# ScalarE's order in the first two groups of a retention and serf-MLP kernel, and the place of one chunk's masks

## The chip, the cores and the metric

The kernel runs on one core of one Trainium2 chip. The metric is the device time of one execution in microseconds (us); the kernel before has a median of 686.3 us over 9 runs (686.1 to 687.0). All times inside an execution are counted from the start of the profiled span.

## The reference

The inputs are q, k and v, each (4, 8, 768, 64): 4 sequences, 8 heads, 768 positions, 64 numbers per head, all float32. For each head with its own decay gamma, a state is updated position by position and read by the query:

```
state = gamma * state + k[t] v[t]^T
y[t]  = q[t] state / sqrt(64)
```

The heads' results side by side form x, with 3072 tokens and 512 columns. Then

```
h = x @ w_in                      # 512 -> 2048
g = h * erf(softplus(h))
out = g @ w_out                   # 2048 -> 512
```

The two weight matrices are float64 on the way in and are converted to float32 on the chip.

## The kernel before

**Chunks.** The retention is computed in 24 chunks of 128 positions (6 chunks in each of 4 sequences). For chunk j, `ret_scale` (K_, line 388) scales k and q with the decays on VectorE, `ret_transpose` (T, line 406) transposes both on TensorE and copies them to SBUF on ScalarE, `ret_scores` (S_, line 427) multiplies them into two PSUM banks, `ret_mask` (M, line 440) applies the causal mask on VectorE, `ret_out` (O_, line 450) multiplies with v and the state and copies the result into xT, and `ret_add` (A, line 606) adds the chunk's part to the state on VectorE. Outside the first stage all the banks called r come from a pool with two buffers: T, S_ and O_ each take both, and each waits until the readers of the one before are done. From chunk 6 on, k and q are loaded in another layout (kq and kb, `load`, line 100) by 32 small transfers and transposed on VectorE (line 413).

**The MLP.** The first 512 tokens (chunks 0 to 3) go through the MLP in groups g = 0 to 3 of four hidden tiles each (ft = 4g + u). `hidden` (line 669) computes one tile of 128 x 512 on TensorE into one of two banks called hp, and copies it to SBUF on ScalarE (line 682); a tile needs the bank of the tile two before it. `gate` (line 619) runs softplus over the group's four tiles, and for g > 0 erf right behind it; for g = 0 `gate_erf` (line 629) is called apart. Each of the two needs a table load on ScalarE. `gated` (line 650) multiplies with h on VectorE, and `project` (line 689) multiplies with w_out. Later tokens go in 256-token chunks through a scheme with seven products instead of eight (`hidden_part`, line 743; `project_part`, line 819); group 4 is the first of these. Its products use two hp banks: products 1, 6, 7 and 4 write the first, products 2, 5 and 3 the second. Product 2 is added to h on VectorE (line 770), and product 5 then overwrites its bank.

**The weights.** They arrive in 16 pieces, in the order in 0, in 1, in 2, in 3, out 0, out 1, in 4, in 5, out 2, out 3, in 6, in 7, out 4, out 5, out 6, out 7 (so piece 4 is out 0, and piece 10 is in 6). `conversion` (line 187) turns a piece into float32: exponent bits on VectorE (line 213), a Relu on ScalarE (line 214), mantissa (217), join with the low word (222), sign and exponent (225), final product (231). Once line 225 has read a piece, the transfer of the piece that takes its place is issued (`load_pieces_after`, line 181): piece 7 behind piece 3, piece 14 behind piece 10, piece 15 behind piece 12. Pieces 0 to 3 are converted in two parts, each of which serves one hidden tile; the others whole, in five steps (213 with 214; 217; 222; 225; 231), and the first step of the next piece goes between the third and the fourth from piece 5 on.

**What sets the order.** The program is written out in order by hand, and each engine and each issuing queue works in that order. Weight steps are put in between by a counter: `pace(n)` (line 277) adds n and issues as many steps as the counter then holds; operations that occupy VectorE subtract from it. `need(...)` (line 285) issues steps until a given weight block is done. The table `after` (line 913) says what follows each hidden tile at once (first list) and what waits until the middle of the next pacing (second list, run by `pace_around`, line 638). After (g, u) = (1, 0) the counter is set to 0. Nearly all transfers are issued from SyncE's queue, in program order: weight pieces, the chunks' loads (`load`), and `load_block_scales` (line 346), 17 small transfers that follow O_ of chunk 5.

Of the kernel before, what the change touches and what calls it, by code (L numbers as in the profile page):

```python
# [22 lines left out]
FG = 4  # L23
# [22 lines left out]
def kernel(  # L46
# [207 lines left out]
    def weights():  # L254


        pending = [conversion(n) for n in range(n_p)]
        begun = 0
        for n, steps in enumerate(pending):
            for k, _ in enumerate(steps, start=begun):  # L260
                yield
                if n > 4 and n + 1 < n_p and k == 2:
                    next(pending[n + 1])
                    yield
            begun = int(n > 4)
            if pieces[n] == ("out", 5):
                yield from sums("in", 0)
# [5 lines left out]
    weight_steps = weights()  # L273
# [11 lines left out]
    def need(*what):  # L285
        nonlocal room
        while what not in done:
            if next(weight_steps, done) is done:
                next(last_steps)
            room -= 1  # L290
# [315 lines left out]
    def ret_add(j):  # L606
        if j not in SU:
            return
        new = SU[j]
        if j % NC:  # L610
            nc.vector.tensor_tensor(state, state, new, op=ALU.add)
        else:
            nc.vector.tensor_copy(state, new)
        pace(-0.4)
# [23 lines left out]
    def pace_around(n):  # L638


        pace(n / 2)
        run(waiting)
        waiting.clear()
        pace(n / 2)
# [14 lines left out]
    def hidden_of(ft, t):  # L659

        if ft not in HP_:
            HP_[ft] = ps_h.tile([P, TCH], F32, name="hp")
        for kk in range(n_k):
            nc.tensor.matmul(  # L664
                HP_[ft][:, t], w_in_of(ft, kk), XC[0][:, kk, t],
                start=(kk == 0), stop=(kk == n_k - 1),
            )

    def hidden(g, u):
        ft = g * FG + u  # L670
        if u == 0:
            HS[g] = act.tile([P, N], F32, name="h")
        need("in", ft)
        if ft == 0:
            hidden_of(1, slice(TCH - C))
        hidden_of(ft, slice(TCH) if ft > 1 else slice(TCH - C, TCH))

        if ft < FG:
            need("in", ft + 2)
        if ft == 0:  # L680
            ret_add(JPC - 1)
        nc.scalar.copy(HS[g][:, u * TCH : (u + 1) * TCH], HP_.pop(ft))  # L682
        done.add(("hidden", ft))
        if ft == FG - 1:
            need("in", FG + 3)
        if g:
            pace_around(3.4 if ft > FG else 0)

# [155 lines left out]
    def put_part(m, step):  # L844
# [27 lines left out]
    K_, T, S_, M, O_, A = (  # L872
        ret_scale, ret_transpose, ret_scores, ret_mask, ret_out, ret_add
    )
# [6 lines left out]
    for j in range(JPC - 2):  # L881
# [3 lines left out]
        if j:  # L885
# [27 lines left out]
    after = [  # L913
        [([], [])] * FG,
        [
            ([(K_, 4), (next, weight_steps), (gate_erf, 0), (load, 5)], []),
            ([], []),
            ([(T, 4)], []),
            ([(S_, 4)], []),
        ],  # L920
        [
            ([(O_, 4)], [(A, 4)]),
            ([(T, 5)], []),
            ([(S_, 5)], [(M, 5)]),
            ([(O_, 5), (load_block_scales,)], [(A, 5)]),
        ],
        [
# [7 lines left out]
    for g in range(G0):  # L935
        for u in range(FG):

            if g and u == (2 if g == 1 else 0):
                waiting.append((gated, g - 1))
            hidden(g, u)  # L940
            run(after[g][u][0])
            if (g, u) == (1, 0):
                room = 0.0
            waiting.extend(after[g][u][1])
        gate(g)
        if g:
            for tt in range(TT):
                project(g - 1, tt)
                if g == 1 and tt < 2:
                    waiting.append((K_, 5) if tt else (M, 4))  # L950
                elif g == G0 - 1 and tt == 0:
                    waiting.extend([(K_, JPC + 2), (T, JPC + 2)])
                elif g == G0 - 1 and tt == 1:
                    load(JPC + 4)
                elif g == G0 - 1 and tt == 3:
                    K_(JPC + 3)
                    T(JPC + 3)
# [129 lines left out]
```

## Time and profile before

| what | value |
|---|---|
| median of 9 runs | 686.3 us (686.1 to 687.0) |
| profiled execution, its own time | 686.28 us |
| its span | 684.6 us |
| PE (TensorE matmul) busy | 677.0 us, 99% |
| PEld (TensorE weight load) busy | 578.3 us, 84% |
| DVE (VectorE) busy | 389.4 us, 57% |
| ACT (ScalarE) busy | 255.7 us, 37% |
| POOL (GpSimd) busy | 5.7 us, 1% |
| granted TensorE clock | 1.0 |
| chain that ended last | PE 90%, DVE 7%, issue 2%, ACT 1% |

A line of the timeline has the start in us, the time of the group, the engine, the source line, the operation, the tiles written and read with their shapes, and the number of instructions; in square brackets stands how long the engine stood idle before it, and what ended that. SPq is SyncE's issuing queue. Instructions on one engine overlap a little, so the distance from start to start is shorter than the sum of durations. Between 25 and 93 us VectorE is busy nearly without a break with the conversion of the weights; PE is busy except for a few holes.

### The profile page before, as it was taken

The page shows a single profiled execution, that of the slowest core. Times are in us where ns is not written, and L with a number is a line of the kernel's source. Part 1 is how long each engine was busy: PE and PEld are TensorE (multiplying, and loading weights), DVE is VectorE, ACT ScalarE, POOL GpSimd, SP SyncE. Part 2 cuts the span into 40 slices and gives each one's busy share as a digit, 9 for nine tenths or more (in the row PEclk, how much of TensorE's full clock was granted, in tenths as well). Part 3 has the DMA queues.
Part 4 walks back from the last instruction along what each step waited for, and adds up shares of the span by engine and source line. Part 5 has one row for each costly group of instructions (what it writes and reads, how often), then busy time and mean ns, then how long its engine had stood idle before and what let it go on. Part 6 is the DMA issues. An engine that isn't in the chain of part 4 may idle for free.

```text
span 684.6 us, 14442 instructions
## 1 busy us (share of the span) xinstructions
PE 677.0 (99%) x6214; PEld 578.3 (84%) x6214; DVE 389.4 (57%) x609; ACT 255.7 (37%) x291; POOL 5.7 (1%) x21
## 2 busy tenths in 40 slices
PE   9999999999999999999999999999999999999998
PEld 8744544586999999999999999999999999999996
DVE  4899999475945644543663564455544554343224
ACT  3368362415324234144143242341441432423431
POOL 2000000100000000000000000000000000000000
PEclk9999999999999999999999999999999999999999
DMA  9999743333412222221231222222312200000000
GB/s 193 214 237 256 181 139 90 63 60 61 108 35 43 75 41 39 74 44 33 66 56 33 65 44 45 70 41 44 72 35 47 51 27 1 2 32 1 1 32 32
DMA packets 156529, 47.65 MB, mean 70 GB/s; under 512 B 143025, under 2 KB 147377, under 8 KB 156465
## 3 DMA queue, kind: packets, MB, share of 16 engines
q1 hardware_dynamic: 153952, 46.19, 31.3%
q10 hardware_dynamic: 2512, 0.53, 0.5%
q8 instruction: 49, 0.80, 0.5%
q14 instruction: 16, 0.12, 0.1%
HBM read 40.39 MB, written 6.29 MB: 68 GB/s over the span
## 4 chain that ended last, share of the span: by engine, by line
PE 90%; DVE 7%; issue 2%; ACT 1%; POOL 0%; DVEq 0%; POOLq 0%
PE hp L757 37%; PE o L829 36%; PE o L700 6%; PE hp L664 3%; PE r L543 1%; PE hp L508 1%; PE o L579 1%; PE o L377 1%; DVE w_out_sb L217 1%; DVE w_out_sb L225 1%; DVE w_out_sb L222 1%; PE r L431 1%; DVE w_in_sb L225 1%; PE hp L558 1%; DVE w_in_sb L231 1%
## 5 line engine op out<-in xcount | busy, mean ns | idle before, releaser
L757 PE MATMUL hp<-xs,w_in_sb 128*128 128x128 f32 x1280 | 149.7, 275 | 0.0
L757 PEld LDWEIGHTS hp<-xs,w_in_sb 128*128 128x128 f32 x1280 | 147.8, 192 | 1.6 <-issue 0.5
L829 PE MATMUL o<-w_out_sb,h 128*128 128x256 f32 x640 | 141.7, 379 | 0.0
L829 PEld LDWEIGHTS o<-w_out_sb,h 128*128 128x128 f32 x640 | 121.6, 190 | 16.5
L757 PE MATMUL hp<-xT,w_in_sb 128*128 128x128 f32 x960 | 113.7, 275 | 0.0
L757 PEld LDWEIGHTS hp<-xT,w_in_sb 128*128 128x128 f32 x960 | 111.9, 192 | 1.9 <-issue 1.0
L829 PE MATMUL o<-w_out_sb,e 128*128 128x256 f32 x480 | 112.1, 383 | 0.0
L653 DVE TENSOR_TENSOR e<-h,e 128x1024 f32<-128x1024 f32 x42 | 49.6, 1221 | 101.7 <-ACT e L634 101.7
L829 PEld LDWEIGHTS o<-w_out_sb,e 128*128 128x128 f32 x480 | 88.2, 190 | 11.6
L664 PE MATMUL hp<-xT,w_in_sb 128*128 128x512 f32 (+2 forms) x144 | 57.2, 550 | 1.2 <-ACT h L682 1.2
L782 DVE TENSOR_TENSOR h<-h,hp 128x512 f32<-128x512 f32 x20 | 13.7, 687 | 75.1 <-PE hp L757 75.1
L624 ACT ACT_TABLE_LOAD x24 | 30.8, 1283 | 60.8 <-issue 45.4
L664 PEld LDWEIGHTS hp<-xT,w_in_sb 128*128 128x128 f32 x144 | 25.6, 190 | 28.5 <-issue 23.8
L634 ACT ACTIVATE e<-e 128x2048 f32<-128x2048 f32 (+1 forms) x23 | 42.1, 1836 | 0.2
L624 ACT ACTIVATE e<-h 128x2048 f32<-128x2048 f32 x22 | 42.0, 1910 | 0.2
L775 ACT COPY h<-hp 128x512 f32<-128x512 f32 x20 | 11.7, 585 | 61.1 <-PE hp L757 61.1
L780 ACT COPY h<-hp 128x512 f32<-128x512 f32 x20 | 11.7, 585 | 60.3 <-PE hp L757 60.3
L770 DVE TENSOR_TENSOR h<-h,hp 128x512 f32<-128x512 f32 x20 | 13.7, 685 | 35.7 <-PE hp L757 35.7
L773 ACT COPY h<-hp 128x512 f32<-128x512 f32 x20 | 11.7, 585 | 57.1 <-PE hp L757 57.1
L634 ACT ACT_TABLE_LOAD x24 | 30.8, 1283 | 0.4
L597 ACT COPY xT<-r 128x256 f32<-128x256 f32 x32 | 10.4, 375 | 54.8 <-PE r L543 54.8
L768 ACT COPY h<-hp 128x512 f32<-128x512 f32 x20 | 11.7, 587 | 48.6 <-PE hp L757 48.6
(136 smaller groups left out, 673.0 us busy)
## 6 DMA issues: line engine op xcount, KB each, us to landing
w_out_sb<-in_moe_w_out_dram SPq DMA_DIRECT2D x14, 512.0 KB, 5.1
kq<-in_k_dram SPq DMA_DIRECT2D x23, 256.0 KB, 3.8
v<-in_v_dram SPq DMA_DIRECT2D x23, 256.0 KB, 3.3
out_dram<-r SPq DMA_DIRECT2D x23, 256.0 KB, 2.9
kq<-in_q_dram SPq DMA_DIRECT2D x288, 16.0 KB, 1.8
kb<-in_k_dram SPq DMA_DIRECT2D x288, 16.0 KB, 1.7
w_in_sb<-in_moe_w_in_dram SPq DMA_DIRECT2D x8, 512.0 KB, 9.5
w_out_sb<-in_moe_w_in_dram SPq DMA_DIRECT2D x8, 256.0 KB, 8.9
```

Of the source, the lines that this page charges most:

```text
L225: nc.vector.scalar_tensor_tensor(power, hi, 1 << 31, power, op0=ALU.bitwise_and, op1=ALU.bitwise_or)
L624: nc.scalar.activation(E[g], HS[g], AF.Softplus)
L634: nc.scalar.activation(E[g][:, half], E[g][:, half], AF.Erf)
L653: nc.vector.tensor_tensor(E[g][:, half], HS[g][:, half], E[g][:, half], op=ALU.mult)
L664: nc.tensor.matmul(HP_[ft][:, t], w_in_of(ft, kk), XC[0][:, kk, t], start=(kk == 0), stop=(kk == n_k - 1),)
L700: nc.tensor.matmul(O[0][tt].rearrange("p (d c) -> p d c", d=2), E[g][:, u * TCH + tt * P : u * TCH + (tt + 1) * P], w_out_of(ft), start=(f ...
L757: nc.tensor.matmul(bank[:, u, :], w_in_sb[:, s, IN[a], kk, u * P : (u + 1) * P], XS[m][b][:, kk, :], start=(p in (1, 2, 5) and u == 0 and ...
L768: nc.scalar.copy(h["11"], flat)
L770: nc.vector.tensor_tensor(h["11"], h["11"], flat, op=ALU.add)
L773: nc.scalar.copy(h["12"], flat)
L782: nc.vector.tensor_tensor(h["12"], h["12"], flat, op=ALU.add)
L829: nc.tensor.matmul(O[m][i][:, half, :], G[g][a][:, u * P : (u + 1) * P], w_out_sb[:, s, OUT[b], u, :], start=i not in started, stop=(s == ...
```

## The change

Three edits of order; no instruction is added or taken out.

- After tile 3, `need` asks for the weights of tile 6 and not of tile 7. The second part of piece 3 (the weights of tile 7) is converted later: `need("in", 7)` stands behind the scaling of chunk 4, after tile 4. On ScalarE softplus of group 0 is now ahead of the Relu of that part.
- One weight step that stood behind the scaling of chunk 4 is dropped there (it comes with a later pacing), and erf of group 0 follows tile 5 instead of tile 4.
- The masks of chunk 5 follow its scores at once, and not in the middle of the pacing of tile 11.

```
         if ft == FG - 1:
-            need("in", FG + 3)
+            need("in", FG + 2)
...
         [
-            ([(K_, 4), (next, weight_steps), (gate_erf, 0), (load, 5)], []),
-            ([], []),
+            ([(K_, 4), (need, "in", FG + 3), (load, 5)], []),
+            ([(gate_erf, 0)], []),
             ([(T, 4)], []),
             ([(S_, 4)], []),
         ],
         [
             ([(O_, 4)], [(A, 4)]),
             ([(T, 5)], []),
-            ([(S_, 5)], [(M, 5)]),
+            ([(S_, 5), (M, 5)], []),
             ([(O_, 5), (load_block_scales,)], [(A, 5)]),
         ],
```

More of the change, by code (lines that the diff above doesn't have):

```diff
@@ L684, in hidden @@
         if ft == FG - 1:
-            need("in", FG + 3)
+            need("in", FG + 2)
         if g:
@@ L915 @@
         [
-            ([(K_, 4), (next, weight_steps), (gate_erf, 0), (load, 5)], []),
-            ([], []),
+            ([(K_, 4), (need, "in", FG + 3), (load, 5)], []),
+            ([(gate_erf, 0)], []),
             ([(T, 4)], []),
@@ L923 @@
             ([(T, 5)], []),
-            ([(S_, 5)], [(M, 5)]),
+            ([(S_, 5), (M, 5)], []),
             ([(O_, 5), (load_block_scales,)], [(A, 5)]),
```

## The prediction

> **What bounds the kernel now.** I read the page first: PE busy 99% of the span, and the chain that ended last is 90% PE, 7% DVE, 1% ACT. So time is lost only where PE stands still. The waits of PE from 22 us to 93 us have three entries: L664 on ACT's copies at L682 (1.2 us, twice), L431 on qT (0.8, before the change begins) and L471 on VectorE's masks at L443 (0.4, twice). After 93.19 us PE waits for nothing that the list shows, up to the end. Then I read the timeline, ScalarE first:
>
> ```profile
> 44.63 0.72 ACT L214 ACTIVATE w_in_sb<-w_in_sb,below 128x512 uint32<-128x512 uint32 x1 [2.01 <-DVE w_in_sb L213]
> 45.37 1.28 ACT L624 ACT_TABLE_LOAD   x1
> 46.66 1.91 ACT L624 ACTIVATE e<-h 128x2048 f32<-128x2048 f32 x1
> 48.48 0.57 ACT L682 COPY h<-hp 128x512 f32<-128x512 f32 x1
> 48.95 1.15 ACT L214 ACTIVATE w_out_sb<-w_out_sb,below 128x1024 uint32<-128x1024 uint32 x1
> 50.11 1.28 ACT L634 ACT_TABLE_LOAD   x1
> 51.41 1.92 ACT L634 ACTIVATE e<-e 128x2048 f32<-128x2048 f32 x1
> 53.23 1.05 ACT L682 COPY h<-hp 128x512 f32<-128x512 f32 x2
> ```
>
> The Relu of the last first-group weights (w_in piece 3, part 1) stands ahead of softplus; the copy of hidden tile 4 stands behind softplus, that of tile 5 behind erf. PE's side:
>
> ```profile
> 49.10 3.70 PE L664 MATMUL hp<-xT,w_in_sb 128*128 128x512 f32 x8 [1.06 <-ACT h L682]
> 52.64 1.04 PE L418 MATMUL r<-ident,kq 128*128 128x128 f32 x8
> 53.85 3.70 PE L664 MATMUL hp<-xT,w_in_sb 128*128 128x512 f32 x8 [0.17 <-ACT h L682]
> 57.48 1.16 PE L431 MATMUL r<-qT,kT 64*128 64x128 f32 x16
> ...
> 90.97 0.43 PE L471 MATMUL r<-qT,state 64*64 64x128 f32 x2 [0.23 <-DVE am L443]
> 91.57 0.66 PE L471 MATMUL r<-qT,state 64*64 64x128 f32 x14 [0.17 <-DVE am L443]
> ```
>
> Ends of matmuls are modelled and overlap, so I measure the loss from start to start. Tile 6 could start at 47.9 (tiles 1 to 5 run without a hole from 29.63 for 18.41 us, less the overlap of about 0.15 that later groups show): **1.2 lost**. T(4) to tile 7 takes 1.21 where T(5) to tile 10 takes 0.87: **0.34**. Tile 7 to S(4) takes 3.63 against 3.53: **0.1**. Tile 11 (87.05) to the end of L471 (92.16) takes 5.11, where 3.53 + 0.60 would do (75.93 to 76.53 in O(4)): **0.98**. In all 2.6 us.
>
> Last I read what PE's next partners do, since a PE that runs earlier meets them:
>
> ```profile
> 136.91 0.69 DVE L400 TENSOR_TENSOR kb<-kb,kq_b 128x512 f32<-128x512 f32 x1 [8.79 <-DMA kb<-in_k_dram]
> ...
> 139.34 0.65 DVE L770 TENSOR_TENSOR h<-h,hp 128x512 f32<-128x512 f32 x1
> 139.92 2.34 DVE L653 TENSOR_TENSOR r<-h,r 128x1024 f32<-128x1024 f32 x2
> ```
>
> VectorE waits 8.79 us for chunk 7's kb, then scales and transposes, then does L770, which reads the second hp bank of group 4. Product 5, whose matmuls overwrite that bank, starts on PE at 141.03. L770 ends at 139.99: **the slack is 1.0 us**, and it is the smallest I found behind 93 us. That kb comes off SyncE's queue, which issues without a pause:
>
> ```profile
> 89.09 0.88 SPq L174 DMA_DIRECT2D w_in_sb<-in_moe_w_out_dram  x2
> 90.01 8.87 SPq L350 DMA_DIRECT2D kq_b<-decay_k_dram  x16
> 98.92 0.43 SPq L354 DMA_DIRECT2D by_b<-decay_s_dram  x1
> 100.14 0.90 SPq L174 DMA_DIRECT2D w_out_sb<-in_moe_w_out_dram  x2
> 101.14 0.41 SPq L113 DMA_DIRECT2D kq<-in_k_dram  x1
> ```
>
> **Part 1: need 6 in place of 7, need 7 after K(4).** No instruction is added or removed; the five VectorE steps and one Relu of piece 3, part 1 move behind softplus and K(4), and the two loads of piece 7 that hang on them (46.28 on SP) move with them, with load(5) still behind. Softplus then follows the Relu of part 0 (41.89, 0.72): table 42.63, softplus 43.92, copy of tile 4 at 45.74 (1.82 after it, as at 48.48). PE needs that copy at 47.9, so the 1.2 goes. VectorE: K(4) at 44.17, piece 3's L213 at 45.30, its L222 at 46.08; its Relu waits for the copy and runs 46.21 to 46.93, so L225 starts at 46.97, not 46.69, and piece 4's L213 at 48.30 instead of 48.03: **+0.27 on VectorE**. Tile 7 needs these weights only at 52.3. Piece 7 is issued at 47.7, lands by 60.1 (12.4 as in this window), is read at 63: hidden, with 3 us left.
>
> **Part 2: the weight step dropped from (1,0), erf behind tile 5's copy.** The step is not lost: the pacing counter is set to 0 after (1,0), so each later place issues the same number of steps, and the whole sequence of weight steps runs one step late against everything else. Applied to the kernel before, this count gives VectorE's order in the trace exactly. ScalarE: copy of tile 5 at 48.06, Relu of piece 4 at 49.02 (behind L213), table 50.18, erf 51.48 to 53.40. gated(0) thus starts at 53.44 against 53.50, though one step less stands ahead of it: VectorE waits 0.29 there. Tile 5 is copied by 48.6, so the 0.34 goes; kT and qT are out by 54.9, as no Relu stands ahead of them. PE: tile 6 at 47.9, T(4) 51.44, tile 7 52.31, S(4) 55.84, project(0) at 56.93 instead of 58.57, and gated(0) (first half 54.7, second 55.8) is in time. Lead 1.64.
>
> A rule speaks against parts 1 and 2. The Trainium skill, "ScalarE: Activation LUTs", section "What ACT_TABLE_LOAD costs", adds about 1.38 us of drain to each switch of sets; here the load lasts 1.28 and softplus starts 1.29 after it, so the trace shows none. By the page tile 4's copy would come at 47.1, still before 47.9.
>
> **Part 3: M(5) right behind S(5).** The two masks pass three weight steps (piece 11's L213, piece 10's L225 and L231). VectorE, re-added with the start-to-start distances of the trace, is 0.32 late here (0.27 + 0.29, less 0.24 where M(4) and A(4) now fill gaps between dependent steps). So M(5) starts at 87.55 instead of 90.24 and ends at 88.83. But PE pays once before: T(5) takes the bank that A(4) (L611, 80.77 before) reads. A(4) now ends at 80.77 (80.36 + 0.41); PE would be there at 79.92 and starts T(5) at 80.81, a **new wait of 0.9**. S(5) at 85.2, tile 11 at 86.3, O(5) at 89.83 with the masks done, project(1) at 91.46 against 93.19. **Lead 1.7** (2.6 less 0.9).
>
> **What takes it back.** Piece 10's L225 releases piece 14's loads (89.09 on SP). It is now behind the masks: 1.20 + 0.32 = 1.5 later. The 18 issues behind it (kq_b, by_b) follow, so by_b ends at 100.86; 0.77 of slack ahead of piece 15's load (100.14) absorbs half, and load(6), load(7) and chunk 7's kb move by **0.75**. (Piece 15's own trigger is only 0.43 late.) L770 then ends at 140.74 and product 5 starts at 140.79 against 141.03. Behind it PE stays ahead of gated(3) (143.0 against 144.5) and of the rest. So of 1.7 us 0.24 remains: 686.28 - 0.24 = **686.0**, with 1.7 us between span and time as now (686.28 against 684.6). The profiled execution stands at the median of 686.3.
>
> The Trainium skill, "Perfetto Trace Analysis", section "Optimization Strategies", advises shortening what PE idles for. Taken alone that gives 684.6; the row at 136.91 with its slack of 1.0 gives 686.0.
>
> **Bounds of what no row shows.** The shift of SP's stream: at least about 0.2 (VectorE meets none of my waits and is 0.24 early: 1.20 - 0.24 - 0.77), so at most 0.8 gained; at most about 1.6 (VectorE 1.2 us late instead of 0.32, the length of two masks), so up to 0.6 lost. I take 0.75, which is re-added from rows. Loads of pieces 7 and 8 while the DMA engines are full (share over 1 until 72 us): nothing, to at most the 1.4 us by which the issue moves; I take nothing, since no VectorE row between 22 and 135 us waits for them.
>
> **Rivals.**
> - *The lead reaches the end.* It needs the kb chain to be no later than before and L770 not to hold product 5; PE's wait list, empty behind 93 us, speaks for it, the 8.79 us wait against. 686.28 - 1.7 = 684.6. Chance 0.08.
> - *Slower: SP's stream is later than PE's slack.* Place: piece 14's loads behind the masks of chunk 5. Each us that kb comes later than 1.0 is lost in full at product 5. With VectorE 1.2 late instead of 0.32 the stream is 1.6 late: 686.9; with VectorE 2.4 late, 2.8: 688.1. It decides from a piece-10 L225 ending 1.77 later than its 89.06; I have 1.5, so the margin is thin. Chance 0.14, half of it past 0.2%.
> - *It does not do what it says*: softplus stays late, or PE is held by the same copies: 686.3. Chance 0.06.
> - *Forecast*, product 5 held by L770 with a shift of 0.2 to 1.3: 685.5 to 686.6, likeliest 686.0. Chance 0.72.
>
> The range leaves out the full lead and the worst of the slower case: 685.1 to 687.0. 0.2% is 1.4 us, about what a measurement of this kernel can tell from no change: faster 0.08, same 0.85, slower 0.07.
>
> **What would show it.** Softplus near 43.9 and no wait at tiles 6 and 7; T(5) waiting for L611 near 80.8; masks near 87.6 and no wait at L471; project(1) near 91.5; piece 14's loads near 90.6, load(6) near 101.9, L400 near 137.7; product 5 waiting for L770. It is wrong if L400 starts no later than 137.0, or if PE runs through product 5 without a wait.

## The result, and the profile after

The changed kernel is **slower**: 689.49 us median of 9 runs (688.87 to 690.23) against 686.19 us for the kernel before (29 runs). The ratio is 1.0048, with a 95% interval of 1.0040 to 1.0057. The profiled execution took 689.08 us with a span of 687.4 us, 2.8 us more than the span before (684.6). Single runs of one kernel lie up to 4 us apart below, with a lower mean granted TensorE clock in the longer ones, and that is part of what is told.

The edits did what they were meant to do on PE. These are PE's lines from the timeline of the changed kernel (start, time, engine, line, what; in brackets PE's idle time and who ended it):

```profile
29.43 21.85 PE L664 MATMUL hp<-xT,w_in_sb 128*128 128x384 f32 x64
51.11 1.04 PE L418 MATMUL r<-ident,kq 128*128 128x128 f32 x8
51.99 3.60 PE L664 MATMUL hp<-xT,w_in_sb 128*128 128x512 f32 x8
...
80.66 0.66 PE L418 MATMUL r<-ident,kq 128*128 128x128 f32 x4 [0.47 <-DVE state L611]
...
89.41 0.67 PE L471 MATMUL r<-qT,state 64*64 64x128 f32 x16
...
91.03 14.00 PE L700 MATMUL o<-w_out_sb,r 128*128 128x512 f32 x32
...
137.78 1.16 PE L431 MATMUL r<-qT,kT 64*128 64x128 f32 x16
142.22 5.47 PE L757 MATMUL hp<-xs,w_in_sb 128*128 128x128 f32 x32 [3.27 <-DVE h L770]
147.52 3.60 PE L700 MATMUL o<-w_out_sb,r 128*128 128x512 f32 x8
```

The lines of the kernel before that these are compared with, PE's and one of SyncE's queue:

```profile
93.19 14.00 PE L700 MATMUL o<-w_out_sb,r 128*128 128x512 f32 x32
...
141.03 3.84 PE L757 MATMUL hp<-xs,w_in_sb 128*128 128x128 f32 x32
144.71 3.60 PE L700 MATMUL o<-w_out_sb,r 128*128 128x512 f32 x8
```

```profile
127.82 7.55 SPq L95 DMA_DIRECT2D kb<-in_k_dram  x16
```

Tiles 1 to 6 now run as one block of 64 matmuls, tile 7 follows T(4) without a hole, and L471 takes 0.67 us in one piece. project(1) starts at 91.03; before it was 93.19, so PE is 2.16 us ahead (0.2 of it from an earlier start of the block, 29.43 against 29.63). Then PE stands still for 3.27 us ahead of product 5, and the two products behind the stop take 5.30 us (142.22 to 147.52) where they took 3.68 (141.03 to 144.71). VectorE shows what it waited for:

```profile
139.08 0.69 DVE L400 TENSOR_TENSOR kb<-kb,kq_b 128x512 f32<-128x512 f32 x1 [10.75 <-DMA v<-in_v_dram]
...
141.51 0.65 DVE L770 TENSOR_TENSOR h<-h,hp 128x512 f32<-128x512 f32 x1
```

and SyncE's queue shows a part of why:

```profile
90.41 0.88 SPq L174 DMA_DIRECT2D w_in_sb<-in_moe_w_out_dram  x2
91.34 9.21 SPq L350 DMA_DIRECT2D kq_b<-decay_k_dram  x16
100.59 0.43 SPq L354 DMA_DIRECT2D by_b<-decay_s_dram  x1
101.12 0.90 SPq L174 DMA_DIRECT2D w_out_sb<-in_moe_w_out_dram  x2
102.12 0.41 SPq L113 DMA_DIRECT2D kq<-in_k_dram  x1
...
128.93 7.54 SPq L95 DMA_DIRECT2D kb<-in_k_dram  x16
136.52 0.43 SPq L122 DMA_DIRECT2D v<-in_v_dram  x1
137.05 1.27 SPq L113 DMA_DIRECT2D kq<-in_k_dram  x1
```

Piece 14's loads come 1.32 us later, load(6) 0.98 us, chunk 7's kb 1.11 us (127.82 before). L400 is later than that, by 2.17 us: the last kb transfers now took 3.0 us from issue to landing, against 1.9 before. (The bracket names v; the last kb transfer, issued at 136.04, landed 3.0 us later, at 139.04, so it is kb that ended the wait.)

The rest is the clock. In this table by stretches the columns are the stretch, its length, the busy time of PE, PEld, DVE, ACT and POOL with their counts, the clock granted to TensorE (1.00 is full speed), the DMA share and GB/s:

```profile
141.00:142.00 1.00, 0.00 (x0) 0.00 (x0) 1.00 (x2) 0.00 (x0) 0.00 (x0) 1.00 0.23 37
142.00:143.00 1.00, 0.78 (x7) 0.79 (x8) 1.00 (x2) 0.00 (x0) 0.00 (x0) 1.00 0.24 37
143.00:144.00 1.00, 1.00 (x8) 1.00 (x7) 1.00 (x2) 0.00 (x0) 0.00 (x0) 0.56 0.23 36
144.00:145.00 1.00, 1.00 (x7) 1.00 (x7) 1.00 (x3) 0.00 (x0) 0.00 (x0) 0.50 0.21 33
145.00:146.00 1.00, 1.00 (x6) 1.00 (x6) 1.00 (x3) 0.00 (x0) 0.00 (x0) 0.50 0.24 37
146.00:147.00 1.00, 1.00 (x9) 1.00 (x8) 0.97 (x2) 0.00 (x0) 0.00 (x0) 0.73 0.21 33
147.00:148.00 1.00, 1.00 (x9) 0.76 (x8) 1.00 (x1) 0.28 (x1) 0.00 (x0) 1.00 0.21 33
```

Nearly a microsecond after PE is back at work its clock is halved, for about 3.4 us. The sum closes on the profiled execution: product 5 starts 1.19 us later than before (142.22 against 141.03), the clock costs 1.62 (5.30 less 3.68), together 2.81, and the span grew by 2.8.

### The profile page after: what moved, and what is told of

Its sections match the earlier page's. It is cut to its first block, busy times and chain, and to the rows that moved or that the text cites. A ratio compares the mean times of both kernels' runs of the same rounds, so it can differ in the third digit from the quotient of the medians.

```text
span 687.4 us, 14444 instructions
## 1 busy us (share of the span) xinstructions
PE 677.6 (99%) x6214; PEld 579.6 (84%) x6214; DVE 389.5 (57%) x609; ACT 256.0 (37%) x291; POOL 5.7 (1%) x21
## 4 chain that ended last, share of the span: by engine, by line
PE 83%; DVE 6%; SPq 5%; issue 3%; DMA 2%; ACT 2%; POOL 0%; ACTq 0%; DVEq 0%; POOLq 0%
PE hp L757 36%; PE o L829 36%; SPq L95 4%; PE o L700 2%; PE r L543 1%; PE hp L508 1%; PE o L579 1%; PE hp L664 1%; PE o L377 1%; DMA kq<-in_k_dram 1%; DMA w_in_sb<-in_moe_w_out_dram 1%; DVE w_in_sb L225 1%; DVE w_out_sb L225 1%; PE r L431 1%; PE hp L558 1%
## 5 line engine op out<-in xcount | busy, mean ns | idle before, releaser
L757 PE MATMUL hp<-xs,w_in_sb 128*128 128x128 f32 x1280 | 151.3, 277 | 3.3 <-DVE h L770 3.3
L757 PEld LDWEIGHTS hp<-xs,w_in_sb 128*128 128x128 f32 x1280 | 149.4, 194 | 4.9 <-DVE h L770 3.5
L770 DVE TENSOR_TENSOR h<-h,hp 128x512 f32<-128x512 f32 x20 | 13.7, 685 | 35.7 <-PE hp L757 35.7
```

Of the source, the lines that this page charges most:

```text
L757: nc.tensor.matmul(bank[:, u, :], w_in_sb[:, s, IN[a], kk, u * P : (u + 1) * P], XS[m][b][:, kk, :], start=(p in (1, 2, 5) and u == 0 and ...
L770: nc.vector.tensor_tensor(h["11"], h["11"], flat, op=ALU.add)
```

## The experiments

**Theory.** PE's lead is real, but SyncE's stream and with it chunk 7's kb come later, so PE stops at product 5; the stop costs its length and then the clock. **Rival:** the changed order costs the time by itself, on ScalarE or through the weight steps that run one step late.

**1. ScalarE's order alone.** The changed kernel with the masks back in the pacing:

```
-            ([(S_, 5), (M, 5)], []),
+            ([(S_, 5)], [(M, 5)]),
```

> The two edits of ScalarE's order alone; the masks of chunk 5 stay in the pacing of tile 11. Theory (the loss comes from the masks ahead of piece 10's L225, which make SyncE's stream and chunk 7's kb late, while PE comes early to product 5): SyncE's stream moves by about 0.4 us at most, the masks stay near 90.5 so that PE's lead is given back at L471, product 5 waits at most a few tenths, no clock drop: 686.0 to 686.8. Rival (the order on ScalarE and the weights running one step late cost the time by themselves): 689, with the loss there although the masks are in their old place.

Measured: 689.34 us, ratio 1.0043 (1.0031 to 1.0055). The number is the rival's, and my expectation was wrong; the trace says why. Piece 14's loads are at 89.54, as good as in their old place, but piece 15's are at 101.71 (100.14 before), because of this VectorE line:

```profile
100.45 1.23 DVE L225 SCALAR_TENSOR_TENSOR w_out_sb<-w_out_sb 128x1024 uint32<-128x1024 uint32 x1 [0.99 <-ACT w_out_sb L214]
```

Piece 12's Relu stands on ScalarE behind softplus and erf of group 2. One step late is enough for that: its step now comes behind the gate of group 2 in the program, and before it came ahead of it. The Relu ran at 99.28, straight behind erf. In the changed kernel the same Relu also stands behind erf, but 1.24 us earlier (98.04), and no VectorE line waits for it. So the order on ScalarE alone makes SyncE's stream late by another way, load(6) at 102.70, and in the profiled run PE stops 1.75 us at product 5, with the clock halved behind it (one of the five runs, 688.16 us, has a mean clock of 1.0):

```profile
140.00:142.00 2.00, 0.30 (x6) 0.11 (x2) 2.00 (x5) 0.00 (x0) 0.00 (x0) 1.00 0.51 100
142.00:143.00 1.00, 0.95 (x5) 0.95 (x6) 1.00 (x1) 0.00 (x0) 0.00 (x0) 0.68 0.21 33
143.00:144.00 1.00, 1.00 (x7) 1.00 (x6) 1.00 (x2) 0.00 (x0) 0.00 (x0) 0.50 0.22 34
144.00:145.00 1.00, 1.00 (x7) 1.00 (x7) 1.00 (x3) 0.00 (x0) 0.00 (x0) 0.50 0.24 38
145.00:146.00 1.00, 1.00 (x7) 1.00 (x7) 1.00 (x2) 0.00 (x0) 0.00 (x0) 0.62 0.23 35
```

Whether the order does harm without the late stream is told by experiment 8.

**2. The masks alone.** The kernel before with `([(S_, 5), (M, 5)], [])`.

> The masks of chunk 5 at once, alone; ScalarE's order as in the kernel before. Theory: PE's lead at project(1) is 1.0 us (the hole ahead of L471 closes), piece 14's loads come 1.2 us later, SyncE's stream 0.45 us later; product 5 waits 0.4 us to 1.5 us (the more, the later the last kb transfer lands), and no clock drop since the stop is short: 685.6 to 686.8. Rival (ScalarE's order is the cause): also near 686, so it is told apart by the run with that order alone; if this run is near 689, the masks alone do it, without the lead of the first part.

Measured: 689.49 us median of 11 runs, ratio 1.0036 (1.0023 to 1.0049), in two bands: three runs of 686.12 to 687.10 with a mean granted clock of 1.0, and eight of 689.33 to 690.29 with 0.997 to 0.998. Two runs of the lower band lie in the expected range, the profiled one and the eight of the upper band above it: the expectation missed. The profiled run (687.10) is of the lower band, with piece 14's loads at 90.72, a stop of 1.21 us at product 5 and no clock drop. The mean clock of the upper band points to a drop, which was not expected; none of its runs has a profile, so how long PE stopped there is open.

**3. The changed kernel with SyncE's stream moved up.**

```
-            ([(O_, 4)], [(A, 4)]),
+            ([(O_, 4), (load_block_scales,)], [(A, 4)]),
...
-            ([(O_, 5), (load_block_scales,)], [(A, 5)]),
+            ([(O_, 5), (load, 6)], [(A, 5)]),
...
-            ([(load, 6)], []),
-            ([(load, 7)], []),
+            ([(load, 7)], []),
+            ([], []),
```

> The changed kernel with SyncE's stream moved up: the 17 block-scale transfers follow the output of chunk 4, and the loads of chunks 6 and 7 each stand one place earlier. Theory: chunk 7's kb lands some 8 us earlier, VectorE does not wait at L400 past 130 us, product 5 follows the scores of chunk 6 without a stop, the clock stays at 1.0, and PE's lead of 2.0 to 2.2 us reaches the end: 683.9 to 684.5. Rival (the loss is not SyncE's stream but the changed order itself, or another wait comes in its place): 686 or more.

Measured: **684.16 us**, ratio 0.9968 (0.9955 to 0.9981), five runs within 0.25 us. The kb of chunk 7 is there 7 us earlier than in the changed kernel, and product 5 follows the scores (PE first, then VectorE):

```profile
137.76 1.16 PE L431 MATMUL r<-qT,kT 64*128 64x128 f32 x16
138.85 3.84 PE L757 MATMUL hp<-xs,w_in_sb 128*128 128x128 f32 x32
142.53 3.60 PE L700 MATMUL o<-w_out_sb,r 128*128 128x512 f32 x8
```

```profile
131.83 0.69 DVE L400 TENSOR_TENSOR kb<-kb,kq_b 128x512 f32<-128x512 f32 x1 [1.68 <-DMA kb<-in_k_dram]
```

This is a kernel that beats both. It also gives the price list of the changed kernel: 684.09 (its profiled run) + 3.27 of stop + 1.62 of clock = 688.98, and 689.08 was measured.

**4. Products 5 and 7 of group 4 change places.** SyncE's stream is as late as in the changed kernel.

```
-        hidden_part(g, 5)
-        hidden_part(g, 7)
+        if first:
+            hidden_part(g, 7)
+            hidden_part(g, 5)
+            add_product_5(g)
+        else:
+            hidden_part(g, 5)
+            hidden_part(g, 7)
```

`add_product_5` is the addition on VectorE that stood behind product 7 and now follows product 5.

> The changed kernel, in which group 4 computes product 7 ahead of product 5 (its addition follows product 5); SyncE's stream is as late as in the changed kernel. Theory: PE has 1.8 us of work that needs no L770, so it stands still for 1.5 us and not 3.3, the granted clock stays at 1.0, and project(0) of group 3 starts near 144.5 instead of 147.5: 686.0 to 686.8, that is 3 us less than the changed kernel although only 1.8 us of work were moved. Rival (the clock drop has another cause than the length of the stop): the clock drops again and it is 687.5 or more.

Measured: 686.16 us (11 runs, 685.78 to 686.71), ratio 0.9997 (0.9988 to 1.0005): 3.3 us less than the changed kernel, from 2.0 us of work put into the stop. Between the two profiled runs it is 3.05 us: 1.45 of a shorter stop and 1.62 of clock. PE still waits 1.82 us for product 2's addition, but the clock stays up:

```profile
140.00:142.00 2.00, 0.74 (x7) 0.55 (x5) 2.00 (x5) 0.58 (x1) 0.00 (x0) 1.00 1.15 230
142.00:143.00 1.00, 0.43 (x3) 0.43 (x4) 1.00 (x2) 0.00 (x0) 0.00 (x0) 1.00 0.24 37
143.00:144.00 1.00, 1.00 (x11) 1.00 (x10) 1.00 (x2) 0.00 (x0) 0.00 (x0) 1.00 0.23 36
```

All 11 runs have a mean clock of 0.999 or 1.0. So the profiled run kept the clock behind a stop of 1.82 us, and that of experiment 1 lost it behind 1.75 us. What stands just ahead of the stop differs (2.0 us of product 7 here, 1.1 us of chunk 6's scores there); whether that decides was not tried.

**5. The kernel before with the stream moved up** as in experiment 3.

> The kernel before with SyncE's stream moved up in the same way (block scales behind the output of chunk 4, the loads of chunks 6 and 7 one place earlier). Theory: in the kernel before product 5 does not wait, so an earlier kb gives nothing: 686.0 to 686.4. Rival (the earlier loads themselves are the gain of the combined version): near 684.2, as much as with the changed order.

Measured: 686.35 us, ratio 1.0000 (0.9991 to 1.0009). The earlier loads alone give nothing.

**6 and 7. The kernel before with a late kb.** Five or nine small transfers ahead of chunk 7's loads, into a tile that nothing reads:

```
+        for i in range(5 if j == 7 else 0):
+            nc.sync.dma_start(
+                extra[:, i], decay_k[:, i % H : i % H + 1].rearrange("(a p) h -> p (a h)", p=32)
+            )
```

> The kernel before with 5 more transfers of 0.5 KB ahead of chunk 7's loads (decay numbers into a tile that nothing reads; about 0.55 us of SyncE's queue each, as the block scales take). Theory: kb comes 2.8 us later, 1.0 us of that is slack, so PE stands still for 1.8 us at product 5: 688.0 with the clock at 1.0 behind it, or 689.7 if a stop of that length already halves the clock for some 3.4 us. Rival (the late kb is harmless, the changed order costs the time): 686.3.

> The kernel before with 9 such transfers ahead of chunk 7's loads. Theory: kb comes 5.0 us later, PE stands still for 4.0 us at product 5, and the clock is halved behind it: 690.3 from the stop and 1.6 to 1.8 from the clock, 691.9 to 692.1. If the clock stays at 1.0, 690.3. Rival (the late kb is harmless): 686.3.

Measured with five: 687.55 us, ratio 1.0031 (1.0016 to 1.0046); eight runs at 687.24 to 687.57 with clock 1.0, four at 690.74 to 691.36 with 0.997 to 0.998. The transfers took 0.5 us each, and the kb stream starts 2.06 us later, not 2.8; the profiled run (687.49) stops 1.43 us, so about 0.6 to 1.0 us of the delay was slack (2.06 less 1.43, or by L400, which is 2.43 us later here, 2.43 less 1.43). Of the gap between the bands, 3.5 us, about half fits the clock: a mean of 0.9975 over 689 us is some 1.7 us lost, an estimate. What the other half is stays open, since no run of the upper band has a profile. Measured with nine: 692.93 us (four runs), ratio 1.0095 (1.0082 to 1.0108), above what I expected. PE stops 4.54 us, and the clock is at half for some 6.8 us, from about 144.8 to 151.6:

```profile
144.50:145.00 0.50, 0.00 (x0) 0.00 (x0) 0.50 (x2) 0.00 (x0) 0.00 (x0) 0.74 0.54 77
145.00:150.50 5.50, 5.08 (x24) 5.08 (x25) 5.47 (x7) 0.00 (x0) 0.00 (x0) 0.50 0.22 34
...
151.50:152.00 0.50, 0.50 (x6) 0.50 (x5) 0.00 (x0) 0.00 (x0) 0.00 (x0) 0.93 0.22 34
```

So a late kb alone, with the old order everywhere else, makes the same kind of loss, a stop at product 5 and the half clock behind it. The rival "the late kb is harmless" falls.

**8 and 9. Each part alone with the stream moved up.** Experiments 1 and 2 with the edit of experiment 3.

> ScalarE's order alone (masks of chunk 5 in their old place), with SyncE's stream moved up as in the combined version. Theory: with kb early nothing stops PE at product 5, and what this part is worth by itself shows: PE is 0.9 us ahead at project(1) in the run of this part with the late stream (92.38 with tiles 1 to 5 at the same start, against 93.19), so 685.3 to 685.6. Rival (this part is harmful in itself): 686.3 or more.

> The masks of chunk 5 at once alone, with SyncE's stream moved up. Theory: the hole of 1.0 us ahead of the output of chunk 5 is closed and reaches the end: 685.2 to 685.5; the clock stays at 1.0 in all runs, where the same kernel with the late stream fell into two bands of 686.1 to 687.1 and 689.3 to 690.3. Rival (the two bands come from the masks' place and not from the stop at product 5): two bands again.

Measured: ScalarE's order 685.26 us, ratio 0.9983 (0.9974 to 0.9992); the masks 685.30 us, ratio 0.9986 (0.9977 to 0.9995), in one band of 685.07 to 685.69. Each part is worth 1.0 to 1.1 us against the 686.33 of the same chip, together what experiment 3 gains. The rival falls: neither order does harm by itself. (The profiled run of the first, 686.38, is the longest of its 11; T(5) waits 1.47 us for L611 in it, and why longer than elsewhere is open.)

**10. The state's addition of chunk 4 at once**, on top of experiment 3: `([(O_, 4), (A, 4), (load_block_scales,)], [])`.

> The changed kernel with SyncE's stream moved up, and the state's addition of chunk 4 at once behind its output instead of in the pacing of tile 9. Theory (the transposes of chunk 5 wait for that addition, 0.5 us by the wait list and some 0.7 us from start to start): PE starts T(5) without a stop and project(1) comes up to 0.7 us earlier, which reaches the end: 683.3 to 683.8. Rival (the hole only moves, to the masks of chunk 5 or to the next addition): 684.1 or more.

Measured: **683.79 us**, ratio 0.9961 (0.9949 to 0.9973), the fastest of all. T(5) runs in one piece (tile 10 starts 0.87 us behind it, as in the kernel before) and PE's wait for L611 is gone. From the start of the block of tiles to project(1) PE takes 61.00 us, against 61.56 in experiment 3. The median is 0.37 us below that of experiment 3, but the two ran on different chips and the intervals of their ratios overlap, so the gain in time is not shown as firmly as the gain in the trace.

**11. The block scales alone moved up**, in the changed kernel.

```
-            ([(O_, 4)], [(A, 4)]),
+            ([(O_, 4), (load_block_scales,)], [(A, 4)]),
...
-            ([(O_, 5), (load_block_scales,)], [(A, 5)]),
+            ([(O_, 5)], [(A, 5)]),
```

> The changed kernel with the block scales alone moved up (behind the output of chunk 4); the loads of chunks 6 and 7 keep their order. Theory: load(6) then waits only for piece 15's trigger (L225, near 100.4) and starts 1.6 us earlier than in the changed kernel, chunk 7's kb is out by 134.5 and lands near 136.4, ahead of the instruction fetch at 136.5; product 5 waits 0.5 to 0.8 us, no clock drop: 684.6 to 685.1. Rival (the late landing of kb has another cause than its issue, for example the load of the queue as a whole): kb lands 1 us later than that, the stop is 1.6 us or longer, 685.7 or more, with runs near 688 when the clock drops.

Measured: 688.06 us (686.56 to 690.24), ratio 1.0026 (1.0014 to 1.0038). A miss. I had left out piece 15's own issues (0.9 us), so load(6) starts at 101.40, 0.72 and not 1.6 us earlier; and the slowest of the last kb transfers again takes 3.0 us to land. VectorE's L400 is at 138.54, PE stops 2.74 us, and the clock drops in the profiled run. Three runs (686.56 to 686.70) kept clock 1.0. By the number and the late landing this is the rival's case: kb is issued 0.7 us earlier, and L400 starts 0.54 us earlier, not the 2 us or more that were expected.

## Why the prediction was wrong

The forecast was 686.0 us with a range to 687.0; 689.49 was measured. Step by step:

- **Parts 1 to 3 on PE: right.** Softplus at 43.72 (forecast 43.92), tile 6 without a hole, S(4) at 55.52 (55.84), the masks at 87.37 (87.55), T(5) held by L611, project(1) at 91.03 (91.46). The lead was 2.0 to 2.16 us instead of 1.7, since only the second half of T(5) waits for L611; that costs 0.69 us (1.56 from T(5) to tile 10 instead of 0.87), not 0.9.
- **"What takes it back": right in mechanism, mis-sized in its first term.** SyncE's stream moved by 1.11 us at chunk 7's kb instead of 0.75. The way was the one forecast (piece 14's loads behind the masks, the block scales behind them), and piece 14's loads were even a little earlier than forecast (90.41 against 90.6); but the 16 block scales took 9.21 us instead of 8.87.
- **"L770 then ends at 140.74": this failed.** I moved L400 with the issue of its transfers and took the time to landing as fixed. It grew by 1.1 us; L770 ended at 142.16. Issue (0.36 more than forecast) and landing (1.07) together make the 1.43 us by which product 5 missed its forecast start (142.22 against 140.79). The bound I gave for the shift was one of the issue alone.
- **The price of the stop: the step that was missing.** My own numbers held a stop of 1.5 us at product 5 (PE ready at 141.03 - 1.73 = 139.30, L770 done at 140.79), and I priced it by its length alone, as if a PE that waits costs only the wait. The clock behind it costs 1.62 us in the profiled run. With 0.36, 1.07 and 1.62 the forecast's 686.04 becomes 689.09; the profiled execution took 689.08.
- **"Slower: SP's stream is later than PE's slack"** is the rival whose outcome came true, at its place, with a chance of 0.14. Its deciding point was not reached: piece 10's L225 ended at 90.39, 1.33 us later than before and not 1.77, and by the forecast's sum kb would then have been within the slack. The slower block scales and, above all, the late landing took it past. With the landing and the clock in its price it would have read 689.

The Trainium skill has the rule that I did not weigh: "TensorE: Matmul & The Clock Gate", section "Why this matters for your kernels", warns of gaps of PE above some 3 us, after which the clock falls to half. The trace shows the half clock and its 3.4 us. It does not show 3 us as the border: the clock fell behind 1.75 us in experiment 1, and did not behind 1.82 us in experiment 4 and 1.43 us in experiment 6. The same page, section "What's actually happening", has the clock judged by free-running windows of 3.4 us; that fits a drop that falls on some runs of one kernel and not on others, but no run here varied the phase by itself.

What stays open: why the last kb transfers land late in some kernels, what besides its length decides whether a stop is followed by the half clock, and how long PE stopped in the runs of the upper bands of experiments 2 and 6.

## What to carry to other kernels

When a bound engine is made faster, look for the next thing it meets that it does not set itself: here a transfer in a queue that issues without a pause, whose slack was 1.0 us while the gain was 2. A new stop is not priced by its length alone; on TensorE allow for the half clock behind it (1.6 us here, more behind the 4.54 us stop of experiment 7, where it stayed at half for some 6.8 us); the shortest stop that had it behind it here was 1.75 us. Where a change moves what releases a queue, move the transfers up with it: the same edits were worth +3.3 us with the loads in their old place and -2.2 us with the loads moved up (experiment 3 against experiment 5).

## What the runs showed of the hardware

- **The clock.** Stops at product 5 or behind it, and what followed: 1.21, 1.43 and 1.82 us (profiled runs of experiments 2, 6 and 4) with the clock at 1.0; 1.75, 2.74, 3.27 and 4.54 us (experiments 1 and 11, the changed kernel, experiment 7) with the clock at 0.50, for 3.4 us behind each of the first three and for 6.8 us, twice as long, behind the last. The half clock does not set in at a fixed time after the stop: in the changed kernel it begins 0.9 us after PE is back at work (143.1, work from 142.22), in experiment 7 0.7 us before (144.8, work from 145.42). Three of the changed kernel's nine runs (690.13 to 690.23 us) have a mean clock of 0.994 to 0.995, the others 0.998 (688.87 to 689.80), so they lost about twice as much to the clock; the profile is of one of the others.
- **An instruction fetch beside the last transfers.** Each trace holds one transfer of 0.02 MB of the instruction queue q8 near the scores of chunk 6. Where it begins among chunk 7's kb transfers or just behind their issue (the changed kernel in 136.5 to 137.0, experiment 4 in the same, experiment 7 in 137.5 to 138.0, experiment 11 in 135.5 to 136.0) the slowest of these takes 3.0 to 3.3 us to land; in the other nine profiles the slowest of the last ones takes 1.9 to 2.3. A SyncE issue near it also takes longer (1.27 us instead of 0.53 for the load of k in the changed kernel). In experiment 7 it comes some 3 us ahead of the last kb issue: the transfers beside it take 3.3 us, the last ones 1.7 to 1.8 again, and the sixteen issues 9.08 us instead of 7.54. The two go together in all thirteen profiles; that the fetch is the cause was not tried.
